# Warm-up and filler products on TensorE, and three steps of batch 1 moved between engines

## Chip, cores and metric

The kernel runs on one core of one Trainium2 chip. The metric is the device time of one execution in microseconds (us). Engines are named as in the profile: PE is TensorE (PEld its weight loads), ACT ScalarE, DVE VectorE, POOL GpSimd, SP the queue that issues the loads and stores.

## The reference

```python
def _attn_ref(q, k, v):            # 8 batches, 8 heads, 576 positions, 64 wide
    scores = scale * np.matmul(q, k.transpose(0, 1, 3, 2))
    # heads 0-3: the last 32 positions; heads 4-7: every 4th of the last 128
    scores = np.where(masks[None, :, :, :], scores, -1000000000.0)
    scores = scores - np.max(scores, axis=-1, keepdims=True)
    attn = np.exp(scores)
    attn = attn / (np.sum(attn, axis=-1, keepdims=True) + 1e-09)
    return np.matmul(attn, v)

def _moe_ref(x, w_theta, w_tok_r, w_tok_i, w_ch):   # x: attention out, (8, 576, 512)
    theta = x @ w_theta
    zr, zi = x * np.cos(theta), x * np.sin(theta)
    y = np.einsum('ts,bsd->btd', w_tok_r, zr) + np.einsum('ts,bsd->btd', w_tok_i, zi)
    u = x + y
    return u + np.maximum(u @ w_ch, 0.0)
```

## The kernel before

A batch goes through attention in four pairs of heads, and then through three products: angles (`theta0` for batch 0, `theta` later), a token product (`token`) and a channel product (`chan`). These are computed with operands split into a high and a low part, three products for one; ScalarE or VectorE rounds the high part and a subtraction on GpSimd or VectorE gives the low part (`split`, `zsplit`, `x_split`, `residual`). In `x_split` (L594 to L599) VectorE subtracts for pairs 0 to 2 and GpSimd for pair 3.

Attention of a pair: `scores` multiplies blocks of queries by their band of keys into score banks "s" (two of them), in groups of five and four columns of blocks. For batch 0, pairs 2 and 3 of batch 1 and pairs 0 and 1 of batch 2 the mask is added on TensorE (`mask_on_pe`), and `row_max` then takes maxima on VectorE; for batches 1 and 2 it also multiplies them by the negative scale there (L438), and ScalarE's exponentials (L485) read the banks with that as their bias and give the banks back. VectorE inverts the sums, and GpSimd multiplies (L510) to the normalised P. P has to be turned before `pv` multiplies it by the values. In batch 0, `flip` does that: 36 products with a unit matrix in two groups of 20 and 16 (L561), then copies out by VectorE (L536) and ScalarE (L539). From batch 1 on `turn` does it with eight VectorE transposes (L525). Two buffers `pts` alternate between pairs.

The units of batch 0 are eight token products (two halves of positions by four blocks of channels, 27 products each) and eight channel products (12 each). A token unit takes its nine blocks of positions in the order KORD = 0, 4, 1, 5, 2, 6, 3, 7, 8, three products each (L850), and waits for each block's high part `zh` (L644 or L641) and low part `zl` (L646).

The order of work in the opening is computed when the kernel is built. `Order` is a planner: each step is a generator that yields an engine and an estimated cost, or an event to wait for; of the steps that are ready on the engine that is free first, the one with the lowest rank goes next, and `pin` fixes that order in the program. Ranks stand in RANK: of the channel weights 2.1, of the units 2.95, of the scores of batch 1 4.02, of its `pv` and what follows it 8.0 and more. TensorE's order is always fixed by `pe`. From batch 1's own products on (`phase`) TensorE's order is written out: units of one batch, scores and turns of the next.

Loads of the opening go through SP's queue in the planned order: masks, a unit matrix, q and k of four pairs, values, the angle weights (`st_wth`), the token weights (`st_wtk`), q, k and values of batch 1, later the second half of the token weights and the channel weights (`st_wch`). Weights are unpacked on VectorE and ScalarE (`unpack`, L332 to L342) and split (L350 ScalarE, L352 GpSimd).

## Time and profile before

| what | value |
|---|---|
| three runs | 575.98, 577.8, 578.51 us; median 577.8 |
| the profiled execution | 577.82 us, span 576.0 us |
| mean granted TensorE clock | 0.988 |
| PE busy | 550.5 us (96%) |
| PE weight loads busy | 501.6 us (87%) |
| DVE busy | 378.0 us (66%) |
| ACT busy | 345.2 us (60%) |
| POOL busy | 222.2 us (39%) |

The page gives busy times over the whole span, and the opening has other limits than the rest. [...] In the order of time, a line is one instruction or a run of like ones; idle time in front of it stands in brackets, with what ended it. The chain of waits follows the last instruction back to what released each step.

### The profile page before, as it was taken

Reading aid. Unit: us, or ns where it says so; the run is one execution under the profiler, and the core shown is the slowest. Engines: PE = TensorE matmul, PEld = TensorE weight load, DVE = VectorE, ACT = ScalarE, POOL = GpSimd, SP = SyncE. Lnnn points to the kernel's source line nnn. Section 1 sums busy time; section 2 is a strip of 40 time slices with the busy share of each in tenths; the row PEclk is TensorE's granted clock in tenths of the full one; section 3 lists DMA queues with packets and bytes.
Section 4 is the critical chain, followed back from the end, with each engine's and each line's share of the span. In section 5 each row is a group of like instructions: output and inputs, shape, how many; then the busy total and the mean of one; then the engine's idle time right before and its main releaser. Section 6 shows DMA issues by size and latency. Waiting matters only on the chain.

```text
span 576.0 us, 13996 instructions
## 1 busy us (share of the span) xinstructions
PE 550.5 (96%) x5464; PEld 501.6 (87%) x5464; DVE 378.0 (66%) x1156; ACT 345.2 (60%) x939; POOL 222.2 (39%) x206
## 2 busy tenths in 40 slices
PE   5997799999999999999999999999999999999997
PEld 4744688879999899988999899988999899989997
DVE  3879798865666668756776768756775767445112
ACT  1498967768555784369555785359556695266110
POOL 2228855525224352226324253226323353325220
PEclk9999699899999999999999999999999999999999
DMA  8991437601747046540746146550747123321002
GB/s 303 400 368 28 165 105 245 216 0 63 231 150 193 32 162 210 169 127 20 268 143 172 64 148 202 181 136 11 252 146 190 69 83 102 77 89 65 18 1 83
DMA packets 45586, 81.91 MB, mean 142 GB/s; under 512 B 3920, under 2 KB 19024, under 8 KB 45520
## 3 DMA queue, kind: packets, MB, share of 16 engines
q1 hardware_dynamic: 45520, 81.02, 43.7%
q8 instruction: 43, 0.70, 0.5%
q14 instruction: 23, 0.19, 0.1%
HBM read 64.49 MB, written 16.52 MB: 141 GB/s over the span
## 4 chain that ended last, share of the span: by engine, by line
DVE 34%; ACT 30%; PE 25%; issue 5%; POOL 2%; DMA 2%; SPq 0%; ACTq 0%; POOLq 0%; DVEq 0%
DVE pt L525 16%; PE y L850 11%; ACT P L504 11%; PE c L882 6%; PE th L685 3%; DVE P L409 3%; ACT K L698 3%; ACT K L787 3%; DVE xh L599 3%; ACT th L796 2%; ACT zh L644 2%; DVE xq L729 2%; DVE K L789 2%; ACT cos L705 2%; ACT x L581 2%
## 5 line engine op out<-in xcount | busy, mean ns | idle before, releaser
L830 POOL TENSOR_TENSOR u<-x,u 128x288 fp32r<-128x288 f32 x64 | 54.7, 858 | 184.6 <-ACT u L828 184.6
L525 DVE STREAM_TRANSPOSE pt<-P 32x288 f32<-32x288 f32 x224 | 105.1, 469 | 12.0 <-POOL P L510 8.9
L882 PE MATMUL c<-u,late_wc 128*128 128x288 f32 x768 | 110.2, 296 | 2.8 <-DVE x L859 2.8
L882 PEld LDWEIGHTS c<-u,late_wc 128*128 128x128 f32 x768 | 106.0, 188 | 6.8 <-DVE x L859 4.0
L850 PE MATMUL y<-wtkh,zh 128*128 128x288 f32 x288 | 90.3, 314 | 1.1 <-ACT zh L644 1.1
L850 PE MATMUL y<-wtkh,zl 128*128 128x288 f32 x288 | 86.2, 299 | 4.0 <-POOL zl L646 4.0
L646 POOL TENSOR_TENSOR zl<-g,zh 128x512 fp32r<-128x512 f32 x40 | 52.3, 1316 | 97.5 <-ACT zh L644 84.5
L504 ACT ACTIVATE P<-P,mx 128x64 f32<-128x64 f32 x216 | 72.0, 335 | 25.8 <-DVE mx L498 25.8
L850 PE MATMUL y<-wtkl,zh 128*128 128x288 f32 x288 | 85.9, 298 | 0.0
L828 ACT CAST u<-x 128x288 fp32r<-128x288 f32 x64 | 26.9, 429 | 86.2 <-DVE x L825 85.5
L685 PE MATMUL th<-wthh,xh 128*128 128x512 f32 x224 | 74.8, 395 | 0.3 <-DVE g L784 0.3
L850 PE MATMUL y<-late_wt_b,zh 128*128 128x288 f32 x320 | 68.1, 297 | 0.0
L825 DVE TENSOR_TENSOR x<-y,x 128x288 f32<-128x288 f32 x64 | 28.1, 448 | 53.6 <-PE y L850 53.5
L850 PEld LDWEIGHTS y<-wtkh,zl 128*128 128x128 f32 x288 | 55.1, 191 | 4.7 <-POOL zl L646 4.7
L850 PEld LDWEIGHTS y<-wtkh,zh 128*128 128x128 f32 x288 | 54.9, 191 | 4.7 <-ACT zh L644 2.3
L850 PE MATMUL y<-late_wt_a,zh 128*128 128x288 f32 x256 | 56.3, 301 | 0.0
L850 PEld LDWEIGHTS y<-wtkl,zh 128*128 128x128 f32 x288 | 55.1, 191 | 0.3 <-issue 0.3
L510 POOL TENSOR_TENSOR P<-P,sm 128x576 f32<-128x576 f32 x32 | 37.5, 1172 | 41.1 <-DVE sm L508 18.1
L850 PEld LDWEIGHTS y<-late_wt_b,zh 128*128 128x128 f32 x320 | 51.4, 189 | 0.3
L685 PEld LDWEIGHTS th<-wthh,xh 128*128 128x128 f32 x224 | 42.0, 188 | 9.2 <-DVE g L784 0.6
L850 PE MATMUL y<-late_wt_b,zl 128*128 128x288 f32 x160 | 47.4, 296 | 0.0
L581 ACT COPY x<-o 128x576 f32<-128x576 f32 x32 | 29.4, 919 | 28.4 <-PE o L617 19.1
(108 smaller groups left out, 1106.3 us busy)
## 6 DMA issues: line engine op xcount, KB each, us to landing
q<-in_qT_dram SPq DMA_DIRECT2D x32, 576.0 KB, 5.2
va<-in_vw_dram SPq DMA_DIRECT2D x30, 320.0 KB, 3.2
k<-in_kT_dram SPq DMA_DIRECT2D x28, 304.0 KB, 5.5
out_dram<-x SPq DMA_DIRECT2D x28, 288.0 KB, 2.4
vb<-in_vw_dram SPq DMA_DIRECT2D x29, 256.0 KB, 3.8
xd<-xq SPq DMA_DIRECT2D x24, 288.0 KB, 5.1
xn<-xd SPq DMA_DIRECT2D x24, 256.0 KB, 3.4
st_wtk<-in_wtk_dram SPq DMA_DIRECT2D x8, 576.0 KB, 8.8
```

Source lines behind the costliest of these rows:

```text
L409: pin(nc.vector.tensor_tensor_reduce(out=P[:, n], in0=ps[:, n - g0], in1=mskb[:, mask_of(pr, n)], op0=ALU.add, op1=ALU.max, scale=1.0, sca ...
L504: table(nc.scalar.activation(P[:, n], P[:, n], AF.Exp, bias=mx[:, n:n + 1], scale=SCALE, accum_out=sm[:, n:n + 1]))
L510: pin(nc.gpsimd.tensor_tensor(P, P, sm.unsqueeze(2).to_broadcast([128, NJ, BW]), op=ALU.mult))
L525: pin(nc.vector.transpose(pmats[b, pr][k0:k0 + QB, :, hh, QB * e:QB * e + QB], P[p0:p0 + QB, :, QB * o:QB * o + QB]))
L581: pin(nc.scalar.copy(dst, src))
L646: pin(nc.gpsimd.tensor_tensor(lo, z, hi.bitcast(F32), op=ALU.subtract))
L685: pe(nc.tensor.matmul(pt, l, r, start=(n == 0), stop=(n == 3 * NC - 1)))
L825: pin(nc.vector.tensor_tensor(x[:, ts], ps, x[:, ts], op=ALU.add))
L828: pin(nc.scalar.copy(uh[b, d][:, ts], x[:, ts]))
L830: pin(nc.gpsimd.tensor_tensor(ul[b, d][:, ts], x[:, ts], uh[b, d][:, ts].bitcast(F32), op=ALU.subtract))
L850: pe(nc.tensor.matmul(ps, l[:, cs], r, start=(n == 0), stop=(n == 3 * NK - 1)))
L882: pe(nc.tensor.matmul(ps, l[:, cs], r[:, ts], start=(n == 0), stop=(n == 3 * NC - 1)))
```

## The change

Five edits, all for the opening:

- Before anything else VectorE fills a tile `ones`, and TensorE multiplies it by itself 14 times (512 columns each) into a bank that nobody reads. They are ahead of every other product in TensorE's order.
- In the first token unit of batch 0, ahead of the products of block 3 (the seventh of nine), eight such products stand in front of its first product and four in front of its third. They write the bank "v", which is taken for this and given back at the end of the unit. The planner counts no time for any of these products.
- In `row_max` for batches 1 and 2, ScalarE multiplies the maxima by the negative scale in VectorE's place.
- In `x_split` for batch 1, GpSimd subtracts for all four pairs.
- Pairs 2 and 3 of batch 1 are turned by `flip`, with banks "x" and "t", in place of `turn`.

```diff
--- before.py
+++ after.py
@@ -38,7 +38,12 @@
 
 FG0 = {4: ("zl2", "zl6"), 0: ("zl3", "zl7"), 1: ("zh3", "zh7")}
 COS_PSUM, SIN_PSUM = True, True
+WARM_UP = 14
+
+FLIPS = [(0, p) for p in range(NP)] + [(1, 2), (1, 3)]
 KORD = (0, 4, 1, 5, 2, 6, 3, 7, 8)
+
+KEEP_BUSY = {(0, 0, 0, 3, 0): 8, (0, 0, 0, 3, 2): 4}
 TP0 = {4: "s", 0: "s", 1: "x", 2: "t", 3: "s"}
 TP = {4: "t", 0: "s", 1: "s", 2: "t", 3: "s"}
 
@@ -434,8 +439,8 @@
                                         op=ALU.subtract))
             give(*rel)
         else:
-            yield "DVE", 170
-            pin(nc.vector.tensor_scalar(mx[:, g0:g1], mx[:, g0:g1], -SCALE, None, op0=ALU.mult))
+            yield "ACT", 220
+            pin(nc.scalar.mul(mx[:, g0:g1], mx[:, g0:g1], -SCALE))
         signal(key)
 
     def scores(b, pr):
@@ -543,7 +548,7 @@
     def flip(b, pr):
 
         yield None, ("P", b, pr)
-        if pr >= 1:
+        if pr >= 1 and (b, pr - 1) in FLIPS:
             yield None, ("fl", b, pr - 1)
         if b or pr >= 2:
             yield None, ("pv",) + divmod(b * NP + pr - 2, NP)
@@ -591,7 +596,7 @@
         lo, lt = hl[:, S + 64:], hl[:, S:S + 64]
         yield "ACT", act(S)
         pin(nc.scalar.copy(hi, x))
-        on = pr < 3
+        on = pr < 3 and b > 1
         eng, cost = (nc.vector, dve) if on else (nc.gpsimd, pool)
         yield "DVE" if on else "POOL", cost(64)
         pin(eng.tensor_tensor(lt, x[:, FS:], hi[:, FS:].bitcast(F32), op=ALU.subtract))
@@ -845,10 +850,16 @@
             yield None, ("wtk", g, kt // 2)
             zh, zl = zs[b, kt]
             wh, wl = (w[:, HS * (kt % 2):HS * (kt % 2) + HS] for w in wtks[g, kt // 2])
+            if (b, d, g, kt) == (0, 0, 0, KORD[6]):
+                busy = yield from bank("v", "busy")
             yield "PE", 369
-            for l, r in ((zh, wh), (zh, wl), (zl, wh)):
+            for i, (l, r) in enumerate(((zh, wh), (zh, wl), (zl, wh))):
+                for _ in range(KEEP_BUSY.get((b, d, g, kt, i), 0)):
+                    pe(nc.tensor.matmul(busy[0][:, :DM], ones[:, :128], ones, start=True, stop=True))
                 pe(nc.tensor.matmul(ps, l[:, cs], r, start=(n == 0), stop=(n == 3 * NK - 1)))
                 n += 1
+        if b == d == g == 0:
+            give(*busy[1])
         signal(("tk", b, d, g))
         go(residual(b, d, g, ps, rel), RANK["evacuate"])
 
@@ -953,6 +964,12 @@
     EA, LA, LA2 = ([(t, reserve(t)) for t in ts] for ts in (EARLY, LATE, LATE2))
     XH = {p: reserve(f"xh{p}") for p in range(NP)}
     UH = {d: reserve(f"u{d}") for d in range(NC)}
+
+    ones = cp.tile([128, DM], BF16, name="ones")
+    nc.vector.memset(ones, 1.0)
+    busy = ps_v.tile([128, 2 * DM], F32, tag="v", name="busy")
+    for n in range(WARM_UP):
+        pe(nc.tensor.matmul(busy[:, :DM], ones[:, :128], ones, start=True, stop=True))
     od.live = True
     go(first_loads(), 0)
     go(consts(), 0)
@@ -977,7 +994,7 @@
     go(units(0), RANK["units"])
     for p in range(NP):
         go(scores(1, p), RANK["scores1"] + p * RANK["pair"])
-        go(turn(1, p), RANK["scores1"] + p * RANK["pair"])
+        go((flip if (1, p) in FLIPS else turn)(1, p), RANK["scores1"] + p * RANK["pair"])
         go(pv(1, p), RANK["pv1"] + p * RANK["pair"])
     for p in range(2):
         go(scores(2, p), RANK["scores2"] + p * RANK["pair"])
```

## Rows read from the trace of the kernel before

**Rows 1.** Table of stretches, core 0: start:end, length, busy us (instructions) by engine, clock, DMA.

```profile
67.03:82.47 15.44, 14.39 (x152) 13.43 (x151) 12.83 (x30) 11.12 (x42) 9.53 (x8) 0.89 0.16 47
82.47:113.14 30.67, 28.72 (x357) 25.99 (x357) 26.17 (x62) 24.68 (x89) 17.23 (x16) 0.94 0.70 242
113.14:144.28 31.14, 29.79 (x211) 26.40 (x209) 20.40 (x41) 21.99 (x35) 14.68 (x13) 1.00 0.08 29
144.28:576.00 431.72, 425.63 (x4141) 401.87 (x4140) 268.67 (x902) 243.77 (x692) 150.83 (x145) 1.00 0.42 127
```

**Rows 2.** Chain of waits in order of time, from the start: start us, us, what.

```profile
3.53 6.60 DMA first_k<-in_kT_dram
...
10.27 1.35 PE s L468 x20
...
17.47 0.64 PE pT L561 x16
...
23.41 0.82 DVE st_wth L332
```

**Rows 3.** TensorE in order of time: start, us, engine, line, operation, tiles, count.

```profile
18.02 0.80 PE L468 MATMUL s<-first_k,q 128*64 128x64 f32 x20
```

**Rows 4.** Instructions of one tile, st_wth: durations in ns (least, median, most), first and last start.

```profile
L325 SPq DMA_DIRECT2D st_wth<-in_wth_dram x4: 328/328/328, 11.6 to 17.5; - x4
...
DMA to landing us min/median/max: 9.6/9.8/10.1
```

**Rows 5.** TensorE in order of time, first token unit; in brackets idle before, and releaser.

```profile
65.15 0.40 PE L850 MATMUL y<-wtkh,zh 128*128 128x288 f32 x1 [1.10 <-ACT zh L644]
...
66.79 0.40 PE L850 MATMUL y<-wtkh,zl 128*128 128x288 f32 x1 [1.11 <-POOL zl L646]
```

**Rows 6.** Table of stretches, TensorE alone: busy us (products touching the stretch), granted clock, DMA.

```profile
67.82:71.16 3.34, 3.34 (x16) 0.50 0.00 0
71.16:74.50 3.34, 3.34 (x26) 0.99 0.00 0
```

**Rows 7.** Order of time of VectorE, ScalarE and TensorE, 79 to 83 us.

```profile
79.02 0.49 DVE L430 TENSOR_REDUCE mx<-s 128x5 f32<-128x320 f32 x1
...
80.83 0.31 ACT L485 ACTIVATE P<-s,mx 128x64 f32<-128x64 f32 x1 [2.35 <-DVE mx L438]
...
82.47 0.31 PE L424 MATMUL s<-mskb,idb 128*128 128x64 bf16 x5 [1.04 <-ACT P L485]
```

**Rows 8.** TensorE in order of time, 101 to 104 us.

```profile
101.51 0.30 PE L424 MATMUL s<-mskb,idb 128*128 128x64 bf16 x2 [1.95 <-ACT P L485]
...
102.24 1.34 PE L468 MATMUL s<-k,q 128*64 128x64 f32 x20
```

**Rows 9.** TensorE in order of time: token products around a group of twenty score products.

```profile
75.81 0.29 PE L850 MATMUL y<-wtkh,zl 128*128 128x288 f32 x1
...
76.77 0.40 PE L850 MATMUL y<-wtkh,zh 128*128 128x288 f32 x1
```

**Rows 10.** Groups of instructions: transposes (mean ns), the small multiplications, the flips' copies.

```profile
L525 DVE STREAM_TRANSPOSE pt<-P 32x288 f32<-32x288 f32 x224 | 105.1, 469 | 12.0 <-POOL P L510 8.9
...
L438 DVE TENSOR_SCALAR mx<-mx x8: 161/172/1305, 80.5 to 109.5; 128x5 f32<-128x5 f32 x4, 128x4 f32<-128x4 f32 x4
...
L536 DVE COPY pt<-pT x8: 409/445/483, 17.3 to 31.6; 64x320 f32<-64x320 f32 x4, 64x256 f32<-64x256 f32 x4
```

**Rows 11.** Remainders on GpSimd (durations in ns), then order of time, GpSimd and TensorE.

```profile
L599 POOL TENSOR_TENSOR xh<-x,xh x7: 1288/1297/1301, 115.0 to 497.6; 128x512 fp32r<-128x512 f32 x7
...
109.70 2.60 POOL L352 TENSOR_TENSOR late_wc<-st_wch,late_wc 128x512 fp32r<-128x512 f32 x2 [2.27 <-ACT late_wc L350]
...
113.14 1.74 PE L882 MATMUL c<-u,late_wc 128*128 128x288 f32 x12
```

**Rows 12.** TensorE in order of time, 120 to 126 us.

```profile
120.27 0.49 PE L685 MATMUL th<-wthh,xh 128*128 128x512 f32 x1 [0.33 <-DVE g L784]
...
125.11 0.63 PE L759 MATMUL xn<-idt,x 128*128 128x128 f32 x4 [1.02 <-DVE g L750]
```

## The prediction

> **What bounds the kernel now.** I read first the table of stretches [rows 1], then TensorE's order of time inside the opening, then, for each idle spell of TensorE, the order of time of the engine that ended it. Rows 1 show where there is anything to gain. From 144.28 us to the end TensorE is busy 425.63 of 431.72 us and none of that code changes, so the change can move the end only by moving the point at which this last stretch begins. Before it lie a head of 67 us, in which TensorE waits for others, and from 67.03 us three stretches in which it is nearly always busy: 14.39 of 15.44, 28.72 of 30.67 and 29.79 of 31.14 us. In these three, what counts is TensorE's idle time, its work, and its clock, which was granted at 0.89 and 0.94 in the first two. The head is a chain through all engines: a load, scores, maxima, exponentials, flips, angles.
>
> **The change part by part.** The sum goes against the profiled execution, 577.82 us (span 576.0 us and 1.8 us around it), which is also the median of the three runs to a tenth.
>
> *Fourteen products of ones at the start.* TensorE does nothing useful until the first pair of loads is in. The chain of waits shows that the second pair's keys land at 10.13 us and that from there the path runs over scores and flips until 18.11 us: eight TensorE pieces, 6.21 us in all [rows 2]. [...] The fourteen products themselves: the stretch of token products at the lower level held 15 starts of 288 columns in 3.34 us, 0.22 us each, at the higher level 25, 0.13 us each [rows 6]. By columns one product of 512 takes about 0.40 or 0.24 us, so fourteen take 5.5 us at the lower level and 3.3 at the higher. They start when the memset of ones is done, which no row shows; VectorE is otherwise idle there, so it costs nothing by itself. If they begin between 1 and 3 us they end before 8.5 us, later than the first scores could start at worst by 1.5 us; but the second pair waits for its load until 10.13 us in any case, and that covers it. Can the rest of the head keep the lead? The first step behind it that needs new data is the unpacking of the angle weights on VectorE at 23.41 us [rows 2]; the four loads are issued from 11.6 to 17.5 us and land 9.6 to 10.1 us later [rows 4], so from 21.2 to 27.6 us, and VectorE could take them up to some 2 us earlier. Bounds: 0 and -2.5 us, and I take **-1.6 us**, nearer to the chain's end because from there on the loads leave that room.
>
> *Twelve products of ones in the first token unit.* TensorE waits there twice, 1.10 us for ScalarE's high part and 1.11 us for GpSimd's low part [rows 5], and shortly behind the second the clock fell: from 67.82 to 71.16 us it was granted at 0.50 [rows 6]. Eight products take 8 x 0.24 = 1.9 us, four 0.95: together 2.85 us into 2.21 us of waits, some 0.65 us too many at the higher level, and 4.75 - 2.21 = 2.5 us too many at the lower. If the clock stays up, 15 products gain 15 x 0.09 = 1.3 us. So between -0.65 and +2.5 us for TensorE. But what the next pair's scores wait for at 82.47 us is a score bank that ScalarE empties [rows 7], and ScalarE there waits for VectorE, not for TensorE. TensorE's lead of 0.65 us becomes a wait there: **0 us** on the path. This cover is gone only if the bank comes free earlier than TensorE does.
>
> *Maxima on ScalarE.* VectorE finishes the maximum of scores at 79.51 us, but does two transposes before the small multiplication that follows; ScalarE, idle for 2.35 us, begins its exponentials at 80.83, and TensorE waits 1.04 us for the bank [rows 7]. With the multiplication on ScalarE, that engine waits only for the maximum. A ScalarE product of five columns has no row; it lies between nothing and the 0.31 us of an exponential of 64 columns. So the exponentials begin at 79.6 to 79.9, about 1 us earlier: **-1.0 us**. The four remaining groups behave alike, and the longest wait is that at 101.51 us: 1.95 us for the same bank, after which twenty score products took 1.34 us, so the clock had fallen again [rows 8]. On VectorE the maxima of that pair stood behind transposes of pair 3. With these gone as well (below) I expect the whole wait to go, **-1.95 us**, and the fall with it. Its price lies between the 0.54 us of that one group and the 0.06 x 30.67 = 1.8 us that the granted 0.94 leaves out [rows 1]; I take **-1.3 us**, near the middle.
>
> *Two pairs turned by TensorE.* Off VectorE go 16 transposes of 0.469 us, 7.5 us; on it come four copies of about 0.445 us, 1.8 us, and on ScalarE as many [rows 10], in engines that have room in this stretch (26.17 and 24.68 of 30.67 us). But TensorE gets 72 more products in a stretch where it is the bound. A group of twenty score products put between two token products widened their distance from 0.13 to 0.96 us [rows 9], 0.83 us; the groups of 20 and 16 of a pair then cost about 0.83 + 0.83 x 16 / 20 = 1.5, with their joints 1.65 us, and two pairs **+3.3 us**. It is nothing only where it falls into idle time that is already counted. TensorE now also waits, in its own order, for GpSimd's normalised P before the flip and for the copies behind it, with all its later token products queued behind. Four such waits at between 0 and the 1.1 us of rows 5: 0 to 4.4 us; I take **+0.6 us**, since the P of pair 2 needs no more than exponentials that now end earlier.
>
> *Behind 113 us.* TensorE waits 0.33 us and 1.02 us there, both for VectorE, whose first step of the angle chain ran only behind the last transposes [rows 12]. VectorE reaches that point with some 5 us less work: **-1.35 us**; bounds 0 and -1.35.
>
> *Remainders on GpSimd.* Three remainders go there; the large one takes 1.30 us [rows 11], with an eighth more for the 64-column piece 1.46 us, 4.4 us in all. GpSimd is busy 17.23 of 30.67 us [rows 1], so it has the time; the angle products need the result only behind 114 us, and channel products cover them. **0 us**, at worst what the third rival says.
>
> Sum: -1.6 - 1.0 - 1.95 - 1.3 - 1.35 + 3.3 + 0.6 = -3.3 us, so 577.8 - 3.3 = **574.5 us**.
>
> **The rivals.** *The lead is lost in the head.* If the clock falls again while TensorE waits for the second and third pair (about 1.5 us of idle, like the 1.95 of rows 8), or if ScalarE and VectorE don't take up the lead behind 23 us, the 1.6 us is not gained: 576.1 us. For it speaks that the change leaves these engines' work before 67 us as it is.
>
> *More goes than I count.* The head keeps all 2.5 us (0.9 more), the flips meet no wait (0.6) and a third of their products fall into idle time (1.1): 571.9 us.
>
> *Remainders in the way of the channel weights.* The last weight splits run on GpSimd from 109.70 to 112.3 us, and the channel products that read them begin at 113.14 [rows 11]: 0.8 us of slack. Two remainders taken ahead of a split add 2.9 us, so TensorE would wait 2.1 us, and a wait of that length is followed by a low clock (1.3 us, as above): +3.4, so 577.9 us. [...] Against this rival: the order of GpSimd's work is planned, and a split has a better rank than a remainder.
>
> *Late flips, slower.* TensorE reaches a flip more than about 2 us before GpSimd has its P, for each of the two pairs. A wait like that at 101.51 us then stands in front of each flip and the clock falls behind it: 2 x (1.95 + 1.3) = 6.5 us instead of 0.6, and the later angle chain gains nothing (1.35): 574.5 + 5.9 + 1.35 = 581.8 us. For it speaks that the planner places a flip by its estimates and TensorE can't go round it; against it that GpSimd and VectorE get less to wait for.
>
> **How the numbers follow.** The forecast, 574.5 us, gets 0.45, with its own range 572.9 to 576.1; the lost lead 0.18; more than counted 0.12; remainders 0.08; late flips 0.17. A measurement of this kernel can tell about 0.5%, 2.9 us, from no change, so faster is below 574.9 and slower above 580.7 us. Faster: 0.12 and 0.36 of the forecast's 0.45, 0.48. Slower: 0.17. Same: the rest, 0.35. The range 571.5 to 579.5 us takes in all cases but the late flips, with 1.6 us above the third rival for flips that wait less than the fourth one says.
>
> **What would show it.** Right: twenty score products at 10 us take 0.8 us and the first token unit starts 1 to 2 us earlier; no granted 0.50 behind that unit; exponentials right behind the maxima; no wait for a score bank near 100 us and no low clock behind it; the last long stretch begins near 141 us and lasts as long as before. Wrong: a TensorE wait for P or for the copies in front of turned pairs, score products that slow down again between 8 and 13 us, or channel products that wait for their weights.

## The result

The changed kernel takes 579.22 us (median of 12 runs, 578.29 to 579.98) against 577.39 us (12 runs of the kernel before beside it, 575.98 to 578.51): ratio 1.0031, 95% interval 1.0021 to 1.0041. It is 1.8 us slower, inside the forecast's range (571.5 to 579.5) but on the other side of the kernel before than the 574.5 us of the forecast. The profiled execution took 579.93 us, with a span of 578.1 us, 2.1 us more than before. All ratios below are to runs of the kernel before on the same chip, each with its 95% interval; they are not the quotients of the medians, and the two can differ by 0.2%.

The stretches of the changed kernel, cut at the same events as [rows 1] (start:end, length, then TensorE busy, weight loads, VectorE, ScalarE, GpSimd, granted clock as a share of full speed, DMA share, GB/s):

```profile
67.72:82.23 14.51, 12.55 (x149) 11.52 (x148) 11.87 (x27) 11.35 (x44) 9.52 (x8) 1.00 0.23 76
82.23:117.31 35.08, 32.78 (x433) 29.21 (x433) 20.24 (x42) 28.47 (x101) 20.75 (x21) 0.95 0.59 201
117.31:146.51 29.20, 29.20 (x211) 26.30 (x209) 18.87 (x38) 20.28 (x33) 13.73 (x13) 1.00 0.08 31
146.51:578.10 431.59, 425.93 (x4140) 402.02 (x4140) 269.16 (x902) 244.39 (x692) 151.48 (x146) 1.00 0.41 127
```

The last stretch is as long as before, so all of the difference lies ahead of it. The head ends 0.69 us later (67.72 against 67.03). The first stretch is 0.93 us shorter, with the clock granted at 1.00 instead of 0.89. The third is 1.94 us shorter and has no idle time left. The loss is in the second: 35.08 us instead of 30.67, 4.41 us more, where 0.65 was expected.

TensorE of the changed kernel in order of time (start, us, engine, line, operation, tiles, count; in brackets the idle time before and what ended it):

```profile
10.22 0.80 PE L473 MATMUL s<-first_k,q 128*64 128x64 f32 x20 [1.24 <-DMA first_k<-in_kT_dram]
...
12.66 0.45 PE L429 MATMUL s<-mskb,idb 128*128 128x64 bf16 x5 [0.81 <-DVE P L438]
13.04 1.34 PE L473 MATMUL s<-first_k,q 128*64 128x64 f32 x20
...
82.23 0.30 PE L429 MATMUL s<-mskb,idb 128*128 128x64 bf16 x5 [1.01 <-ACT P L490]
...
86.58 0.80 PE L566 MATMUL pT<-idt,P 64*64 64x64 f32 x20 [0.44 <-POOL P L515]
...
99.73 0.31 PE L429 MATMUL s<-mskb,idb 128*128 128x64 bf16 x2
...
109.89 0.69 PE L622 MATMUL o<-pt,vb 128*64 128x64 f32 x16 [1.86 <-DMA vb<-in_vw_dram]
```

In the head the twenty score products of the second pair take 0.80 us (clock granted at 1.00 from 10.20 to 11.10 us), those at 13.04 us take 1.34 us again (granted at 0.50 from 13.00 to 14.40 us), behind waits of 1.24 and 0.81 us. The wait of 1.95 us at the score bank [rows 8] is gone: the scores at 99.73 follow without one. In its place TensorE waits 1.86 us for the second half of a value load (vb). From 110.51 to 117.31 us the clock was then granted at 0.75. The small multiplication on ScalarE took 0.21 us, and the exponentials follow it at once, 0.2 us earlier than in [rows 7] although the head is 0.69 us late:

```profile
80.30 0.21 ACT L443 ACTIVATE mx<-mx 128x5 f32<-128x5 f32 x1 [1.13 <-DVE mx L435]
80.59 0.31 ACT L490 ACTIVATE P<-s,mx 128x64 f32<-128x64 f32 x1
```

The late load is last in a chain. The changed kernel's queue of SyncE, and the unpacking of the channel weights (st_wch) on VectorE:

```profile
92.91 1.20 DVE L337 TENSOR_SCALAR st_wch<-st_wch 128x512 f32<-128x512 f32 x1 [0.39 <-DMA st_wch<-in_wch_dram]
...
94.35 1.46 DVE L337 TENSOR_SCALAR st_wch<-st_wch 128x512 f32<-128x512 f32 x1
...
100.89 1.58 SPq L330 DMA_DIRECT2D st_wch<-in_wch_dram  x2
...
103.05 0.38 SPq L255 DMA_DIRECT2D vb<-in_vw_dram  x1
```

The second pair of weight loads waits for GpSimd's splits of the first pair to free the tiles, and the value load stands behind it in the queue; it landed 6.8 us after its issue, at 109.85 us. The kernel before issued the same load 2.05 us sooner:

```profile
101.00 0.36 SPq L250 DMA_DIRECT2D vb<-in_vw_dram  x1
```

It landed 6.5 us later, at 107.5 us, and the products that read it followed at 108.50 without a wait. So most of what the load lost, it lost before its issue.

### The profile page after: what moved, and what is told of

Read it like the earlier page. It is cut to its first block, busy times and chain, and to the rows that moved or that the text cites. A ratio compares the mean times of both kernels' runs of the same rounds, so it can differ in the third digit from the quotient of the medians.

```text
span 578.1 us, 14189 instructions
## 1 busy us (share of the span) xinstructions
PE 557.6 (96%) x5562; PEld 503.6 (87%) x5562; DVE 370.9 (64%) x1131; ACT 348.1 (60%) x951; POOL 225.5 (39%) x212
## 4 chain that ended last, share of the span: by engine, by line
PE 52%; DVE 21%; ACT 19%; issue 3%; DMA 2%; POOL 1%; SPq 0%; POOLq 0%; DVEq 0%; ACTq 0%
PE y L859 24%; PE c L893 11%; DVE pt L530 9%; PE th L690 8%; ACT P L509 6%; PE o L622 3%; PE s L473 3%; DVE P L414 2%; ACT K L703 2%; ACT K L792 2%; DVE xh L604 1%; ACT th L801 1%; DVE K L794 1%; ACT zh L649 1%; POOL P L515 1%
## 5 line engine op out<-in xcount | busy, mean ns | idle before, releaser
L530 DVE STREAM_TRANSPOSE pt<-P 32x288 f32<-32x288 f32 x208 | 97.5, 469 | 13.4 <-POOL P L515 10.6
L830 DVE TENSOR_TENSOR x<-y,x 128x288 f32<-128x288 f32 x64 | 28.2, 449 | 53.5 <-PE y L859 53.3
```

What stands on the lines that cost most here:

```text
L530: pin(nc.vector.transpose(pmats[b, pr][k0:k0 + QB, :, hh, QB * e:QB * e + QB], P[p0:p0 + QB, :, QB * o:QB * o + QB]))
L830: pin(nc.vector.tensor_tensor(x[:, ts], ps, x[:, ts], op=ALU.add))
```

## The experiments

**First series: one part alone, or one part taken out.** The first theory was that each part has an effect of its own, and that the value load (one buffer, behind the channel weights in SyncE's queue) or the remainders on GpSimd cause the loss. The rival: the stretch from 82 to 113 us is balanced so finely that any shift costs about as much. "Alone" means the changed kernel with the other four parts taken out.

The change with two value buffers:

```diff
-            r = yield from take("vb", 1)
-            vb = ap.tile([128, NJ - VA, 128], F32, tag="vb", name=f"vb{b}_{pr}", bufs=1)
+            r = yield from take("vb", 2)
+            vb = ap.tile([128, NJ - VA, 128], F32, tag="vb", name=f"vb{b}_{pr}", bufs=2)
...
-            go(load_vb(NP if n == NP - 2 else n + 1), RANK["load"])
+            go(load_vb(n + 2), RANK["load"])
+            if n == NP - 2:
+                go(load_vb(n + 3), RANK["load"])
```

> The changed kernel with two buffers for the second part of the values in place of one, so that its load doesn't wait for the pair before. Theory A (the wait of 1.86 us in front of pair 3's products of P and values, and the granted 0.50 behind it, come from that one buffer): the wait is gone, the clock stays at 1.00 there, and the time falls from 579.2 by 1.9 and by up to 1.6 us, to about 576 us, which is 1.4 us below the kernel before. Rival B (something else is late at the same point, the channel weights on GpSimd above all): the wait moves to the first channel products, and the time stays within 1 us of 579.2.

Measured: 1.0066 (1.0048 to 1.0084). The wait for the value load is gone, but TensorE waits 2.42 us for VectorE at 79.72 and 1.61 us for ScalarE at 112.48 instead. Neither theory came out. The planner had made a new order, so this does not tell what the load costs.

The change without the turned pairs of batch 1, and the turned pairs alone (the first edit, and its reverse with the other parts out):

```diff
-FLIPS = [(0, p) for p in range(NP)] + [(1, 2), (1, 3)]
+FLIPS = [(0, p) for p in range(NP)]
```

> The changed kernel with pairs 2 and 3 of batch 1 turned by VectorE again. Theory A (TensorE's 72 products more cost it 3.3 us where it is the bound, and the late products of P and values cost the 1.86 us wait and the low clock): at least 2 us faster than the changed kernel, some 576 to 577 us. Rival B (VectorE's relief is worth more than TensorE's products, and the loss is in the head): slower than the changed kernel, 580 us and more, with the wait for a score bank near 100 us back.

> The kernel before with pairs 2 and 3 of batch 1 turned by TensorE and nothing else of the change. Theory A (as above): the products of P and values of pair 1 come behind the flip of pair 2, the load of the values' second part becomes a chain, and the time is 2 us above the kernel before, about 579.5 us. Rival B (the flips pay by the wait near 100 us that they remove, as the prediction had it, -1.95 -1.3 -1.35 +3.3 +0.6): 576.7 us, and the loss comes from one of the other edits.

Measured: without them 1.0031 (1.0012 to 1.0049), as slow as with them; alone 1.0052 (1.0036 to 1.0069). Without them TensorE waits 1.75 us for a channel-weight split at 115.72, and neither theory fits the time; alone it waits 1.50 us for the value load at 108.33, as theory A had it, but the loss is 3.0 us instead of 2.

The warm-up alone (`WARM_UP = 14`) and the products of ones alone (`KEEP_BUSY` as changed):

> The kernel before with the fourteen products of ones at the start and nothing else of the change. Theory A (the clock falls again while TensorE waits for the second and third pair's loads, and is then low until 19 us in place of 17): the first token unit begins 0.5 to 0.8 us later than in the kernel before, and the time is 0 to 0.8 us above it, about 578 us. Rival B (the recorded execution's fall is an accident and the lead of up to 1.6 us is usual): 575.8 us.

> The kernel before with one edit: the products of ones (8 and 4) in TensorE's waits of the first token unit. Theory A (they keep the granted clock at 1.00 from 68 to 71 us, and the lead of about 1.5 us is taken away again by a later wait for a bank or for the maxima): 577.2 +- 0.8 us, ratio 1.000 +- 0.0015, with a new wait of about 1 us at 78 to 83 us. Theory B (the lead gets through to the channel products): 575.5 us or less. Theory C (balanced stretch: a shift costs a wait and the clock): 578.5 us or more.

Measured: 1.0056 (1.0041 to 1.0071) and 1.0044 (1.0024 to 1.0063). In both, every other instruction stands in the order of the kernel before. The warm-up's loss of 3.2 us is more than either of its theories allowed. Theory C of the second fits its time, but says nothing of why.

The small multiplications on ScalarE alone, the remainders on GpSimd alone, and the change without the remainders:

```diff
-            yield "DVE", 170
-            pin(nc.vector.tensor_scalar(mx[:, g0:g1], mx[:, g0:g1], -SCALE, None, op0=ALU.mult))
+            yield "ACT", 220
+            pin(nc.scalar.mul(mx[:, g0:g1], mx[:, g0:g1], -SCALE))
...
-        on = pr < 3
+        on = pr < 3 and b > 1
```

> The kernel before with one edit: in the first token unit of batch 1 the small product of the maxima with the scale is made by ScalarE instead of VectorE. Theory A (each term of the sum stands by itself): the exponentials of that unit start about 1.0 us sooner, TensorE's wait at 82.47 us shrinks by about 1 us and nothing else moves: 575.5 to 577.0 us, ratio 0.998 +- 0.002. Theory B (the stretch from 82 to 113 us is balanced, so that any shift of it turns into a TensorE wait of over 1.5 us and a low granted clock behind it): 578.5 us or more, and the trace has a wait of TensorE of 2 us or more between 90 and 113 us.

> The kernel before with one edit: the remainders of x of batch 1's tokens are taken by GpSimd instead of VectorE. Theory A (GpSimd's work beside VectorE's unpacking of the channel weights stretches it, and the weight split on GpSimd queues behind the remainders): the unpack of 0.43 and 1.00 us takes 1.2 us or more each, the last weight split on GpSimd comes about 2 to 3 us later than 109.7 us, and the time is 578.5 to 580.5 us, ratio 1.002 to 1.006. Theory B (the remainders are off the path, as the prediction counted them): 577.2 +- 0.8 us, ratio 1.000 +- 0.0015, and the channel products start at 113 us as before.

> The changed kernel with one part undone: the remainders of x of batch 1 are taken by VectorE again. Theory A (the remainders on GpSimd delay the weight split, and behind it in the queue of SyncE the load of the value bias, for which TensorE waits 1.86 us at a low clock after it): VectorE's unpack is back at about 0.43 and 1.00 us, the load is issued about 3 us sooner, the wait of 1.86 us is under 0.7 us, and the time is 576.0 to 577.5 us, about 2 to 3 us under the changed kernel. Theory B (the remainders are off the path): 579.2 +- 0.8 us as with them, with the wait of 1.86 us still there.

Measured: 1.005 (1.0031 to 1.0069), 1.0038 (1.0024 to 1.0052) and 1.0045 (1.0027 to 1.0063). The first edit moves all eight multiplications, not those of one unit only, as its expectation says. With it alone the wait at 82 us is indeed gone, but TensorE waits 1.29 us for a value load at 97.50, and channel products wait three times (theory B's time came, its wait of 2 us did not):

```profile
114.73 0.53 PE L893 MATMUL c<-u,late_wc 128*128 128x288 f32 x2 [0.86 <-ACT late_wc L355]
116.10 0.40 PE L893 MATMUL c<-u,late_wc 128*128 128x288 f32 x1 [0.84 <-POOL late_wc L357]
117.63 0.61 PE L893 MATMUL c<-u,late_wc 128*128 128x288 f32 x1 [1.13 <-DVE x L830]
```

With the remainders alone, a remainder (96.42 to 98.24 us) pushes GpSimd's two weight splits, which began at 96.73 in the kernel before, back to 98.20. A multiplication that took 0.17 us in the kernel before (at 99.67) now falls beside the second split and takes 1.18 us, and TensorE's next scores wait for VectorE's maxima:

```profile
98.20 2.56 POOL L357 TENSOR_TENSOR late_wc<-st_wch,late_wc 128x512 fp32r<-128x512 f32 x2
...
99.61 1.18 DVE L443 TENSOR_SCALAR mx<-mx 128x5 f32<-128x5 f32 x1
...
102.46 0.42 PE L429 MATMUL s<-mskb,idb 128*128 128x64 bf16 x2 [2.98 <-DVE mx L443]
```

Five parts of quite different kinds, and each alone costs 2.2 to 3.2 us; together they cost 1.8. Effects of the parts themselves can't add up like that. Only the remainders' run lies in the range of its theory A, and of its mechanism half came: the last weight split began 3.4 us later (114.36 instead of 110.97), but the two unpacks took 0.57 and 1.04 us, hardly more than before. Without the remainders the wait for the value load stayed at 1.87 us, as theory B had it. The rival, that any shift costs about as much, fits all of these times, but names no cause.

**Second series: the parts without the planner's new order.** The planner plays its estimates through and takes, on each engine, the best-ranked task that is ready; moving one operation changes that play. Compared line by line, the multiplications alone changed some 350 lines of the instruction order, the remainders alone some 170. So the same edits were made with the planner told the old engine and cost; all other instructions then keep the order of the kernel before. Two controls go with them: the changed text with all parts out, and the same with only the memset of the ones.

```diff
             yield "DVE", 170
-            pin(nc.vector.tensor_scalar(mx[:, g0:g1], mx[:, g0:g1], -SCALE, None, op0=ALU.mult))
+            pin(nc.scalar.mul(mx[:, g0:g1], mx[:, g0:g1], -SCALE))
...
-        on = pr < 3
+        on = pr < 3 and b > 1
...
-        yield "DVE" if on else "POOL", cost(FS)
+        yield ("DVE", dve(FS)) if on or pr < 3 else ("POOL", pool(FS))
```

> The changed kernel's text with every part of the change taken out again, so that each engine gets the same instructions in the same order as in the kernel before; only line numbers differ. Theory A (each of the five parts run alone came out 2.3 to 3.2 us slower because of what it changes on the chip): 577.4 +- 0.7 us, ratio 1.000 +- 0.0015. Theory B (something that all the tried kernels share besides their edits makes them slower): 579.5 us or more.

> As the kernel before, in the same order of instructions, with one instruction more: VectorE fills a tile of ones (128x512) at the very start, where it waits for loads anyway. Theory A (what counts is each edit's work and order in the stretch to 113 us): 577.4 +- 0.7 us, ratio 1.000 +- 0.0015. Theory B (any small change of the program, of its length or of where its tiles and instructions lie, is enough to lose the few us by which the kernel before stands out): 579.5 us or more.

> The kernel before with the ten small products of the maxima with the scale in batch 1 made by ScalarE instead of VectorE, but with the planner told the old engine and cost, so that all other instructions stand in the order of the kernel before (in the run with the planner told the new ones, 353 lines of the order differed). Theory A (the part itself saves about 1 us at 82.47 us and the planner's new order lost it): 575.5 to 577.0 us, ratio 0.998 +- 0.002. Theory B (a shift of the stretch by itself costs a wait and the clock, whatever the order): 578.5 us or more.

> The kernel before with the six remainders of x of batch 1 on GpSimd instead of VectorE, with the planner told the old engine and cost, so that all other instructions stand in the order of the kernel before. Theory A (GpSimd's two-input operations make VectorE's small products and unpacks beside them wait, 0.17 us becoming 1.16 us and 0.43 us becoming 1.0 us or more, and push the weight split on GpSimd back): 578.5 to 580 us, ratio 1.002 to 1.005. Theory B (the planner's new order was the cost): 577.4 +- 0.8 us.

Measured: 1.0006 (0.9992 to 1.002), 1.0004 (0.9992 to 1.0015), 0.9988 (0.9975 to 1.0001) and 0.9998 (0.9981 to 1.0014). The controls are as fast as before. The multiplications, 1.005 with the planner's new order, come to 0.9988 with the old one, an interval that only just takes in no change; the remainders go from 1.0038 to 0.9998. For these two parts the cost was the new order, and nothing that can be told from zero was the part: theory A of the multiplications' run stands in direction, theory A of the remainders' run falls, since GpSimd's operations do stretch VectorE's (a multiplication that took 0.17 us in the kernel before takes 1.18 us there too) but the time shows no cost when the order is the old one.

**Third series: rows of TensorE's program.** The warm-up and the products of ones changed no order and still cost over 2 us. What they share is that TensorE's program gets longer, by 28 and 24 rows (each product has a weight load). The trace shows ten packets of 16 KB on an instruction queue of its own (q8) before 145 us, each worth 0.9 to 1.2 us of one of the 16 DMA engines. In the run with the warm-up TensorE twice waits for nothing that the profile shows:

```profile
18.53 0.62 PE L622 MATMUL o<-pt,first_v 128*64 128x64 f32 x14 [1.16 <-issue]
...
24.66 0.67 PE L566 MATMUL pT<-idt,P 64*64 64x64 f32 x14 [0.89 <-issue]
```

Between these two starts 129 products and 128 loads touch the stretch, in this run as in the one with 24 rows below. That these are waits for its program is argued from more such cases: two waits of this kind, 0.89 to 1.66 us long, stand in six of the eight traces with products of ones at the start and in none of the twelve without, and each of the twelve waits ends 1.2 to 1.6 us after a packet on q8 is in. The counts of the pages go with this: the kernel before has 43 packets on q8 (0.70 MB) for 5464 products and as many weight loads, the changed one 44 (0.72 MB) for 5562 and as many, 254 and 253 rows to a packet. So a packet on q8 is taken here for the fetch of the next piece of TensorE's program (the expectations call it a block), and a cut of the program is the point between two pieces. The view calls the queue "instruction" and names no engine. If it is so, more rows ahead of a point move every later cut, and with it the moment of its fetch; the fetch near the channel weights, at 90.2 us in the kernel before, starts at 88.1 and 89.1 us in two runs with 24 rows more and at 82.4 us in one with 156. In the kernel before it comes 4.0 us after the first load of these weights is issued, and the load is in before VectorE wants it (SyncE's queue and VectorE in order of time; the expectations below give the fetches up to 0.25 us too early, as quarters of a us showed them):

```profile
86.22 2.69 SPq L325 DMA_DIRECT2D st_wch<-in_wch_dram  x2
...
91.07 0.43 DVE L332 TENSOR_SCALAR st_wch<-st_wch 128x512 f32<-128x512 f32 x1
```

The fetch is this row of the queues from 90 to 91 us (packets, MB, share of 16 engines; 5.8% of 16 us are 0.93 us):

```profile
q8 instruction: 1, 0.02, 5.8%
```

With the products of ones it starts at 88.1 us, 3.0 us after the issue, and the load is late (the same views, and TensorE's scores):

```profile
85.08 2.71 SPq L330 DMA_DIRECT2D st_wch<-in_wch_dram  x2
...
91.34 0.43 DVE L337 TENSOR_SCALAR st_wch<-st_wch 128x512 f32<-128x512 f32 x1 [1.44 <-DMA st_wch<-in_wch_dram]
...
102.09 0.30 PE L429 MATMUL s<-mskb,idb 128*128 128x64 bf16 x2 [3.67 <-ACT P L490]
```

Two experiments test this: 24 rows that move no work, and the same filling of the waits in pieces that put the cut elsewhere.

```diff
+WARM_UP = 12
...
+    ones = cp.tile([128, DM], BF16, name="ones")
+    nc.vector.memset(ones, 1.0)
+    busy = ps_v.tile([128, 2 * DM], F32, tag="v", name="busy")
+    for n in range(WARM_UP):
+        pe(nc.tensor.matmul(busy[:, :64], ones[:, :128], ones[:, :64], start=True, stop=True))
```

```diff
-KEEP_BUSY = {(0, 0, 0, 3, 0): 8, (0, 0, 0, 3, 2): 4}
+KEEP_BUSY = {(0, 0, 0, 3, 0): 52, (0, 0, 0, 3, 2): 26}
...
-                    pe(nc.tensor.matmul(busy[0][:, :DM], ones[:, :128], ones, start=True, stop=True))
+                    pe(nc.tensor.matmul(busy[0][:, :64], ones[:, :128], ones[:, :64], start=True, stop=True))
```

> The kernel before, in its order, with 12 tiny products of ones (64 columns each, 24 rows of TensorE's program with their weight loads) at the very start, where TensorE waits for loads: they end long before the first load lands, so that no work moves. [...] In the kernel before the block fetched at 90.0 us comes 3.8 us after the first channel-weight load is issued (86.22); in the two runs where TensorE got more rows with the order unchanged (products of ones alone, warm-up alone) it came 2.9 us after it, and the load landed about 1.4 us later. Theory A (the fetch of TensorE's program block, 0.9 us of one DMA engine, lands in the middle of the channel-weight load and holds it up): the block comes 2.5 to 3.2 us after the issue, VectorE's first unpack waits 1 to 1.5 us for the load, the wait for the scores near 101.5 us grows from 1.95 to over 3 us, and the time is 579 to 580.5 us, ratio 1.003 to 1.006. Theory B (those two runs lost by the lead that their products gave): 577.5 +- 0.8 us, ratio 1.000 +- 0.0015.

> As the run with the products of ones alone, but the two waits are filled with 52 and 26 products of 64 columns instead of 8 and 4 of 512: about the same time of TensorE, but 156 rows of its program instead of 24, so that the block fetched in the middle of the channel-weight load comes before that load's issue (at about 84 us). Theory A (the fetch held the load up): no wait of over 0.7 us of VectorE for the first channel-weight load, the wait near 101.5 us is 2.2 us or less again, and the time is 576.3 to 578.0 us, against 580.15. Theory B (the lead itself is what hurts): 579.5 us or more, as with the large products.

Measured: 1.004 (1.0024 to 1.0056) for 24 rows that do nothing, and 0.9998 (0.998 to 1.0017) for the small pieces, against 1.0044 for the large ones. The run with 24 rows in order of time: two waits in the head as in the warm-up's, then the weights' issue, the unpacking and the scores:

```profile
18.81 0.57 PE L622 MATMUL o<-pt,first_v 128*64 128x64 f32 x12 [1.03 <-issue]
...
24.96 0.56 PE L566 MATMUL pT<-idt,P 64*64 64x64 f32 x12 [0.96 <-issue]
...
86.44 2.71 SPq L330 DMA_DIRECT2D st_wch<-in_wch_dram  x2
...
92.37 0.43 DVE L337 TENSOR_SCALAR st_wch<-st_wch 128x512 f32<-128x512 f32 x1 [1.12 <-DMA st_wch<-in_wch_dram]
...
103.12 0.30 PE L429 MATMUL s<-mskb,idb 128*128 128x64 bf16 x2 [3.35 <-ACT P L490]
```

Its fetch, starting at 89.1 us and so 2.7 us after the issue, in the row of the queues from 89 to 90 us:

```profile
q8 instruction: 1, 0.02, 5.5%
```

And its table of stretches around the scores:

```profile
100.00:108.00 8.00, 4.88 (x51) 4.27 (x51) 6.22 (x18) 6.12 (x25) 3.24 (x3) 0.79 0.65 229
```

The clock was granted at 0.79 there, as in the kernel before (below), so it has no part in this loss.

Each point of theory A came as written: the late load, the longer wait at the scores (1.95 before), the time. In the small pieces the fetch starts at 82.4 us and is over before the weights are issued, the load is in time, and the scores wait 2.23 us, just over the 2.2 of theory A:

```profile
85.03 2.70 SPq L330 DMA_DIRECT2D st_wch<-in_wch_dram  x2
...
89.88 0.43 DVE L337 TENSOR_SCALAR st_wch<-st_wch 128x512 f32<-128x512 f32 x1
...
100.59 0.30 PE L429 MATMUL s<-mskb,idb 128*128 128x64 bf16 x2 [2.23 <-ACT P L490]
```

So where the cut falls decides 2.3 to 2.7 us here. The other traces in the order of the kernel before agree. In eight of them the fetch comes 4.0 to 4.6 us after the issue of the first weight load, or is over before it; the load lands 4.5 to 5.0 us after its issue, the scores near 101 us wait 0.8 to 2.9 us, and the ratio is 1.0006 or less. In three (24 rows, warm-up, products of ones) the fetch comes 2.7 to 3.0 us after the issue; the load lands 5.8 to 6.2 us after it, the scores wait 3.4 to 3.7 us, and the ratio is 1.004 or more. That fetch and load meet on one DMA engine is argued from their times; no view names the engine.

Two more runs of this series: the multiplications and the remainders together with the old order, and the whole change with the planner told the old engines and costs for these two (the edits of the second series).

> Two parts of the change, the small products of the maxima on ScalarE and the remainders on GpSimd, with the planner told the old engines and costs, so that all other instructions stand in the order of the kernel before, and TensorE's program has as many rows as before. Theory A (the parts add up when order and rows stay): 576.2 to 577.2 us, ratio 0.998 +- 0.0015, the first version under the kernel before. Theory B (GpSimd's remainders take back what ScalarE's products give): 577.5 us or more.

> The whole change, all five parts, with the planner told the old engines and costs for the products on ScalarE and the remainders on GpSimd; the order is then that of the run with the turns by TensorE alone, with 52 rows more of TensorE's program. Theory A (half of the loss is the planner's new order for these two parts, the other the turns and the blocks of the program): 577.8 to 579.0 us, under the changed kernel's 579.2. Theory B (the planner's order for these two parts is no loss within the whole change): 579.2 to 581 us.

Measured: 0.9979 (0.9963 to 0.9995), faster than before, and 1.0055 (1.0037 to 1.0072). In the first the scores near 101 us wait 0.95 us instead of 1.95, and from 100 to 108 us the clock is granted at 1.00 (table of stretches):

```profile
100.00:108.00 8.00, 6.45 (x93) 5.41 (x93) 4.93 (x13) 5.90 (x27) 5.13 (x6) 1.00 0.88 295
```

The same stretch of the kernel before:

```profile
100.00:108.00 8.00, 6.49 (x64) 5.56 (x65) 6.17 (x17) 5.83 (x27) 2.41 (x2) 0.79 0.75 247
```

Theory A of the second falls: inside the whole change the old order for two parts doesn't help, and TensorE again waits 1.97 us for a value load. That the turned pairs, which have re-planned the stretch anyway, are the reason is not shown.

**Fourth series: what adds up, and the change with other cuts.** The two parts with the old order and the small pieces together; and the whole change, in its own order, with the small pieces as its only edit.

> Products on ScalarE, remainders on GpSimd, both with the order of the kernel before kept, and the products of ones in 52 and 26 small pieces, which put the cuts of TensorE's program where they did no harm in the run with these pieces alone. Theory A (the parts add up once order and cuts are harmless, and the lead of about 1.1 us from the products of ones, taken away at 82 us so far, gets through since the maxima come sooner): 574.5 to 575.8 us, ratio 0.9965 +- 0.0015, under the 575.96 of the two parts alone. Theory B (the lead is taken away at a later wait, at the transposes before the scores near 101 us): 576.0 +- 0.7 us, as without the products of ones.

> The whole change in its own order, with one edit: the products of ones in 52 and 26 pieces of 64 columns instead of 8 and 4 of 512, so that every cut of TensorE's program behind 64 us falls 132 rows sooner. In the changed kernel one block comes at 89.5 us, 1.5 us after the first channel-weight load is issued (87.95), and one at 105.0, 2 us after the issue of the value load for which TensorE then waits 1.86 us. Theory A (these two fetches hold the loads up): the wait for the value load falls under 1 us, the granted clock stays up behind it, and the time is 576.5 to 578.2 us. Theory B (the loads are late by their place in SyncE's queue and by their sum, and the cuts only add noise): the wait stays at 1.5 us or more and the time at 579.2 +- 0.8 us.

Measured: 0.9958 (0.9942 to 0.9974) and 1.0004 (0.9987 to 1.002). The first has the lowest ratio of the study, 2.4 us under the kernel before and, by the two ratios, 4.2 us under the changed one. Its stretches:

```profile
67.50:82.19 14.69, 13.46 (x168) 12.43 (x164) 11.95 (x28) 11.53 (x45) 9.73 (x8) 1.00 0.20 66
82.19:111.61 29.42, 27.59 (x358) 24.88 (x357) 26.07 (x51) 24.62 (x96) 19.36 (x19) 1.00 0.74 245
111.61:142.73 31.12, 29.87 (x211) 26.33 (x209) 19.92 (x41) 22.62 (x35) 16.28 (x16) 1.00 0.08 29
```

Its scores near 101 us, in TensorE's order of time:

```profile
101.10 0.30 PE L429 MATMUL s<-mskb,idb 128*128 128x64 bf16 x2 [0.84 <-DVE pt L530]
```

The clock is granted at 1.00 in all three; the first two stretches are 0.75 and 1.25 us shorter than in [rows 1]. Its two theories are not told apart: the ratio lies in the range of A, but the time of 575.92 us is also that of B, on a chip where the kernel before takes 578.62, and the interval overlaps that of the two parts without the small pieces (0.9963 to 0.9995). The lead of the small pieces is partly taken at 82 us all the same (0.62 us). What they add is therefore not shown.

The whole change with its cuts moved, the stretch that held the loss:

```profile
82.03:114.73 32.70, 31.24 (x433) 27.68 (x432) 18.32 (x41) 27.98 (x101) 19.61 (x20) 1.00 0.65 217
```

And its wait for the value load:

```profile
108.84 0.69 PE L622 MATMUL o<-pt,vb 128*64 128x64 f32 x16 [1.04 <-DMA vb<-in_vw_dram]
```

The stretch is 32.70 us instead of 35.08, the clock 1.00 instead of 0.95 and the wait 1.04 us instead of 1.86. The fetch at 105.0 us, 2 us after the value load's issue, now comes at 99.0, before it, and the load's landing fell from 6.8 to 6.0 us. The fetch at 89.7 us, which followed the first weight load by 1.8 us, now comes 4.4 us behind it, and that load lands 3.5 us after its issue instead of 4.9. The time is that of the kernel before. The wait is just above what theory A allowed, so the load is late partly by its place in the queue; the larger part of the loss, 0.27% or 1.6 us, went with the cuts, and the two intervals just miss each other. By which of the loads is not shown: the value load took 6.5 us in the kernel before with no fetch beside it, so a fetch need not be what made it 6.8.

## Why the prediction was wrong

*Reading of the bound.* Right: the last stretch kept its length (431.59 us), and the end moved with its beginning.

*Fourteen products, -1.6 us.* Wrong; 0. No run shows this term, nor the 2.5 us that bound it: twenty score products near 10 us took 0.80 us in the changed kernel and with the warm-up alone (at 10.22 and 9.93 us), where they took 1.35 before [rows 2] and 0.80 only at 18.02 us [rows 3]; but no earlier end of the head came of it. The first rival named the place: in the changed kernel those at 13.04 us take 1.34 us, at a granted 0.50. In the warm-up's own run those at 12.63 us take 0.80 us, and the lead is gone all the same, with two waits of 1.16 and 0.89 us for TensorE's own instructions. The 24 rows that do no work bring the same two waits. Rows alone don't make them: the two traces with the rows and without the waits (the changed kernel, and the same with small pieces) are those in which the clock fell back. Nor does the clock alone: without the rows there are none, though in the trace with all parts out twenty score products took 0.80 us from 13.33 us on, with no warm-up at all. So the longer score products until 18 us, without which there is nothing for the warm-up to win, are not there in every execution either. The first angle products of block 0 start between 26.5 and 28.2 us in thirteen traces without the warm-up and between 26.9 and 27.8 in seven with it. The changed kernel's later head (27.69 against 27.00) lies inside that spread and is no effect that could be shown.

*Twelve products, 0 us.* Right as far as it went: the clock stayed at 1.00 and the lead became waits of 0.94 us at 78.76 and 1.01 us at 82.23. What was left out is that they are also 24 rows of program; alone, the products cost 2.5 us.

*Multiplications on ScalarE, -1.0 us.* Right: 0.21 us each, and the first stretch is 0.93 us shorter. Alone with the old order the whole part brought 0.7 us (0.9988), in an interval that only just takes in nothing.

*The wait at 101.51 us, -1.95 and -1.3 us.* The step that failed. That wait went as predicted, but a wait of 1.86 us for the value load took its place, and a clock of 0.75 for 6.8 us behind it took the place of the old fall: idle time in the stretch 2.30 us instead of 1.95, mean clock 0.95 instead of 0.94. The prediction took the rest of the order, and the loads in it, as given. The planner's play moved the loads (the value load was issued at 103.05 instead of 101.00 us), and the longer program moved the fetches among them: with the cuts alone moved, the wait fell to 1.04 us and the ratio from 1.0031 to 1.0004. The low clock is not what the loss needs: of the twelve runs of the changed kernel the slowest, 579.98 us, was granted a mean clock of 1.000.

*Turned pairs, +3.3 and +0.6 us.* The work was as sized: products of 0.80 and 0.68 us, four groups, one wait of 0.44 us for P. TensorE's busy time in the three stretches, less the share that the clock held back, rose by 3.4 us (an estimate from the two tables), against 3.3. Whether the turned pairs are worth their 3.3 us stays open: alone they came with a new order and 1.0052.

*Behind 113 us, -1.35 us.* Right: both waits are gone, and the stretch has no idle time.

*Remainders, 0 us.* Right on the path (0.9998 with the old order), though VectorE's operations did take longer beside GpSimd's: 1.18 us instead of 0.17 for a multiplication beside GpSimd's split (remainders alone) and 1.46 us for the unpack at 94.35 of the changed kernel beside a remainder. The unpack at 92.91, 1.20 us, stands beside GpSimd's multiplication of P, which the change does not move; with the small pieces it starts ahead of it and takes 0.39 us.

The sum by stretch, forecast and then measured in the profiled executions: head -1.6 and +0.69, first stretch -1.0 and -0.93, second +0.65 and +4.41, third -1.35 and -1.94, last 0 and -0.13; in all -3.3 and +2.1 us. The miss is in the head (2.3 us) and in the second stretch (3.8 us), where the wait and the clock, 3.25 us, were not won. Of the rivals, the lost lead happened, and a late wait with a low clock behind it as well, but for a load and not for a turned pair. None of them had the order or the program's length as a cost of its own.

*What stays open:* which DMA engine a fetch and a load meet on; how much the turned pairs cost apart from the order they bring; why, with the cuts moved, the change still gains nothing; and what lets the clock fall. The changed text with all parts out waited 2.05 us at the same scores, the remainders with the old order 2.93 us, and both kept a granted 1.00 from 100 to 108 us, where the kernel before, with 1.95 us, was granted 0.79. So the prediction's rule that such a wait brings a low clock, with its 1.3 us, does not hold by itself.

## What to carry to other kernels

Where a planner orders the work, an edit is two changes: the operation, and a new order for everything around it; measure the operation first with the old order kept, because here the new order cost 2 to 4 us for each of two operations, which together gained 1.2 us with the old one. Count the instructions that an edit adds to the busiest engine's program, and look at where its program fetches then fall among the loads that the path waits for. And when several unlike edits each cost the same, stop adding up their parts and run controls: a text with all parts out, and an edit that does nothing but lengthen the program.

## What the runs showed of the hardware

- Twenty-four rows more in TensorE's program, which do no work on the path, cost 2.3 us (1.004) where a fetch (a packet on q8) of 0.9 us comes 2.7 us after the issue of a 512 KB load instead of 4.0: the load then lands 5.8 us after its issue instead of 4.6, 1.1 us late for VectorE. In the three traces with such a fetch it landed after 5.8 to 6.2 us, in the eight without one after 4.5 to 5.0. With the fetch over before the load's issue (small pieces, 156 rows more) the ratio was 0.9998.
- TensorE twice waited for nothing that the profile shows, 1.03 and 0.96 us with 24 rows more, at a DMA share of 1.03 between the two; such waits stand in six traces, 0.89 to 1.66 us long. That they are waits for its program is argued from the times of the packets.
- A wait of TensorE did not settle its clock: the clock stayed at 1.00 behind waits of 2.05 and 2.93 us and was 0.79 around one of 1.95 us at the same scores.
